# A channel mix in groups of four chunks, with the weights as the stationary operand in all three products

## The chip, the cores and the metric

The kernel runs on one core of a Trainium2 chip. The metric is the time of one execution on the device, in microseconds, of which the median of three runs is taken.

## The reference, cut to what matters

Inputs are q, k, v and a gate alpha, each 4 batches x 8 heads x 768 steps x 48 features, in fp32. A gated linear attention makes x (768 steps x 384 features a batch), and a channel mix follows it:

```python
for t in range(S):
    state = alpha[:, :, t, :, None] * state + np.einsum('bhd,bhe->bhde', k[:, :, t], v[:, :, t])
    y[:, :, t] = np.einsum('bhd,bhde->bhe', q[:, :, t], state)
...
x_prev = np.concatenate([np.zeros((B, 1, D)), x[:, :-1, :]], axis=1)
xk = mu_k * x + (1.0 - mu_k) * x_prev
xr = mu_r * x + (1.0 - mu_r) * x_prev
k = np.maximum(xk @ w_k, 0.0)          # 384 -> 1024, "up"
v = k * k @ w_v                        # 1024 -> 384, "down"
r = 1.0 / (1.0 + np.exp(-(xr @ w_r)))  # 384 -> 384, "gate"
return (r * v).astype(np.float32)
```

## The kernel before

The 3072 steps of all batches are cut into 24 chunks of 128 (six a batch). The attention works chunk by chunk, on data that DVE prepares in nine spans (PREP: three of two chunks, six of three): forward and backward scans of alpha (`scan` L826, `scan_back` L843), and products with q and k. On TensorE (PE) a chunk is a `visit`: scores of a later chunk (`sp`, masked by DVE into `am`, L983), transposes (`sp` L992, copied by ACT into `ht`), `intra` (L1023), `updates` (L1035, which DVE adds to the state `st`, L1062) and, for the chunk before, `inter` (L1049), all into the PSUM tile `yu`. ACT copies the result into `xt` (L1094), and SP's queue moves the features of a fourth row block into their place (`move_y3`, L1103).

The channel mix works on groups of chunks (MIX, before: three groups of two chunks and six of three, so 256 or 384 columns). Of a group, ACT and DVE first mix each step with the one before it (`x_mul`, `x_add`) and split the result in a high part (fp32r, by ACT) and a low part (by DVE). Then come, on PE:

- up: for each of eight blocks f of 128 hidden features, three tiles of input features times three factors (high x high, low weights x high, high x low), nine matmuls into one PSUM tile `pk` (L1160). The weights are stationary, the group's columns stream. ACT makes relu, DVE or ACT the square, ACT and DVE its high part `kh` and low part `kl`.
- gate: for each chunk, nine matmuls into `pg` (L1204). Here x is stationary (128 steps) and the 384 output features of the weights stream. ACT makes the sigmoid.
- down: for each chunk, 24 matmuls into `pv` (L1227), k stationary and the weights streaming. DVE multiplies with the sigmoid (`gated`, L1234), and SP stores 128 steps x 384 features (192 KB).

Group 0 (in FULL) is done in plain fp32 with one factor, each matmul as two instructions, while the weights are still being split for the rest. The PSUM tiles of the mix (`pm`) are two. A row of DVE's and ACT's work on a weight is `w_top`, `w_or`, `w_hi`, `w_lo` (L914 to L941).

Nothing is ordered by hand. `graph` builds a list of jobs with what they need and an estimated length; `SPOTS` says how many mix jobs on PE stand ahead of each visit; `Plan.run` sorts the jobs of the other engines by the length of what hangs on them, with an offset by kind and group from the table `SOONER`. The instructions of each engine, and the DMAs on SP's queue, are issued in that order, and each engine works strictly in order.

## Time and profile before

| what | value |
|---|---|
| median of three runs | 340.75 us (340.56 to 340.97) |
| span of the profiled execution | 339.2 us |
| PE busy | 327.1 us, 4552 matmul instructions |
| VectorE (DVE) busy | 242.4 us |
| ScalarE (ACT) busy | 193.5 us |
| mean granted TensorE clock | 0.997 |

The profile is one execution; its span runs from the first instruction of the program to the last, and its instruction times are what all sums below are made of. The median of the runs lies 1.6 us above that span. A busy time of PE counts each matmul from its start to the end of its pipeline, so matmuls in a row overlap, and the chain of work (which follows back what ended last) gives the spacing of matmuls better than their durations do.

### The profile page before, as it was taken

To read this page: it belongs to the slowest core of one execution; us is meant where nothing else is said; L and a number is where in the kernel's file an instruction comes from. 1 tells how busy PE (TensorE), PEld (TensorE's weight loads), DVE (VectorE), ACT (ScalarE), POOL (GpSimd) and SP (SyncE) were. 2 spreads that over 40 slices of the span, in tenths; PEclk is the share of its full clock that TensorE was granted. 3 is DMA by queue.
4 is the path that set the end of the run, shared out by engine and by line. 5 is a ranking of instruction groups with operands and counts; after the bars stand their busy time and mean duration, and the time that the engine had idled before them with its cause. 6 is when DMAs were issued, how large, how long until landed. Compare 5 with 4: busy or idle time off the path is not lost.

```text
span 339.2 us, 10688 instructions
## 1 busy us (share of the span) xinstructions
PE 327.1 (96%) x4552; PEld 307.6 (91%) x4552; DVE 242.4 (71%) x513; ACT 193.5 (57%) x439; POOL 6.8 (2%) x28
## 2 busy tenths in 40 slices
PE   8888999999999999999999999999999999999993
PEld 8777865799999999999999999999999999999992
DVE  4989998998985997788669965893667256627310
ACT  3586773587588396655554564752667167706400
POOL 5000000000000000000000000000000000000000
PEclk9999999999999999999999999999999999999998
DMA  7989493433434232414243215121000000010001
GB/s 225 409 334 278 154 336 95 146 97 131 134 89 163 47 106 85 148 39 137 70 162 79 75 33 182 43 56 52 14 10 23 32 31 9 23 47 2 2 23 53
DMA packets 14325, 35.38 MB, mean 104 GB/s; under 512 B 2432, under 2 KB 9344, under 8 KB 13504
## 3 DMA queue, kind: packets, MB, share of 16 engines
q1 hardware_dynamic: 14016, 33.73, 30.5%
q10 hardware_dynamic: 256, 0.92, 1.0%
q8 instruction: 37, 0.61, 0.7%
q14 instruction: 16, 0.13, 0.1%
HBM read 26.57 MB, written 4.72 MB: 92 GB/s over the span
## 4 chain that ended last, share of the span: by engine, by line
PE 80%; DVE 7%; DMA 6%; ACT 5%; issue 1%; DVEq 0%; ACTq 0%
PE pv L1227 29%; PE pk L1160 25%; PE pg L1204 10%; PE yu L1049 4%; PE sp L975 3%; PE yu L1023 3%; PE sp L992 3%; PE yu L1035 3%; DMA rv<-wv_p 2%; DMA al<-al_p 1%; DMA kq<-kq_p 1%; DVE pp L843 1%; DVE am L983 1%; DMA xt<-xt 1%; ACT xt L1094 1%
## 5 line engine op out<-in xcount | busy, mean ns | idle before, releaser
L1227 PE MATMUL pv<-wvh,kh 128*128 128x384 f32 x176 | 59.7, 339 | 0.2 <-DVE flag L1256 0.2
L1227 PE MATMUL pv<-wvh,kl 128*128 128x384 f32 x176 | 59.5, 338 | 0.0
L1227 PE MATMUL pv<-wvl,kh 128*128 128x384 f32 x176 | 59.3, 337 | 0.0
L1168 ACT ACTIVATE r<-pk 128x384 f32<-128x384 f32 (+1 forms) x72 | 32.6, 452 | 29.0 <-PE pk L1160 27.6
L1160 PE MATMUL pk<-xkh,wkh 128*128 128x384 f32 (+1 forms) x192 | 42.3, 328 | 0.0
L1160 PE MATMUL pk<-xkl,wkh 128*128 128x384 f32 (+1 forms) x192 | 41.4, 324 | 0.0
L1160 PE MATMUL pk<-xkh,wkl 128*128 128x384 f32 (+1 forms) x192 | 41.2, 323 | 0.0
L1193 DVE TENSOR_TENSOR kl<-k,kh 128x384 fp32r<-128x384 f32 (+1 forms) x64 | 33.1, 524 | 10.7 <-ACT k L1174 4.8
L1176 DVE TENSOR_TENSOR k<-r 128x384 f32<-128x384 f32 x48 | 26.6, 556 | 18.7 <-ACT r L1168 18.4
L1189 ACT ACTIVATE kh<-r 128x384 fp32r<-128x384 f32 (+2 forms) x72 | 35.1, 489 | 1.9
L1131 ACT ACTIVATE x<-xt,mu 128x384 f32<-128x384 f32 (+1 forms) x48 | 26.4, 584 | 13.8 <-DVE xkl L1144 11.0
L1227 PEld LDWEIGHTS pv<-wvh,kh 128*128 128x128 f32 x176 | 33.0, 188 | 0.3 <-DVE flag L1256 0.3
L1227 PEld LDWEIGHTS pv<-wvl,kh 128*128 128x128 f32 x176 | 33.1, 188 | 0.0
L1094 ACT COPY xt<-yu 48x256 f32<-48x256 f32 (+1 forms) x72 | 26.7, 371 | 11.1 <-PE yu L1049 10.2
L1227 PEld LDWEIGHTS pv<-wvh,kl 128*128 128x128 f32 x176 | 33.0, 188 | 0.0
L1160 PEld LDWEIGHTS pk<-xkh,wkh 128*128 128x128 f32 x192 | 32.1, 188 | 0.3
L1234 DVE TENSOR_TENSOR sig<-pv,sig 128x384 f32<-128x384 f32 x24 | 13.3, 554 | 26.6 <-PE pv L1227 26.6
L1160 PEld LDWEIGHTS pk<-xkh,wkl 128*128 128x128 f32 x192 | 32.2, 188 | 0.1
L1160 PEld LDWEIGHTS pk<-xkl,wkh 128*128 128x128 f32 x192 | 32.1, 188 | 0.1
L1135 DVE SCALAR_TENSOR_TENSOR x<-xt,nu,x 128x384 f32<-128x384 f32 (+1 forms) x48 | 26.4, 579 | 3.0 <-ACT x L1131 3.0
L826 DVE TENSOR_TENSOR_SCAN pp<-al,tiny 128x384 f32<-128x384 f32 (+2 forms) x28 | 22.7, 847 | 4.1 <-DMA al<-al_p 4.0
L843 DVE TENSOR_TENSOR_SCAN pp<-al,inv 128x384 f32<-128x384 f32 (+2 forms) x28 | 24.9, 914 | 0.0
(89 smaller groups left out, 514.1 us busy)
## 6 DMA issues: line engine op xcount, KB each, us to landing
kq<-kq_p SPq DMA_DIRECT2D x6, 1153.5 KB, 6.2
out<-sig SPq DMA_DIRECT2D x24, 192.0 KB, 1.9
al<-al_p SPq DMA_DIRECT2D x6, 577.5 KB, 4.1
v<-v_p SPq DMA_DIRECT2D x6, 576.0 KB, 4.6
rk<-wk_p SPq DMA_DIRECT2D x4, 768.0 KB, 8.5
rv<-wv_p SPq DMA_DIRECT2D x4, 768.0 KB, 5.2
kq<-kq_p SPq DMA_DIRECT2D x2, 769.5 KB, 8.6
v<-v_p SPq DMA_DIRECT2D x3, 384.0 KB, 8.1
```

What stands on the lines that cost most here:

```text
L826: self.DVE.tensor_tensor_scan(self.pp[g][:, t], self.al[g][:, t, :n], self.tiny[:rows].to_broadcast([rows, n]), initial=START, op0=ALU.mul ...
L843: self.DVE.tensor_tensor_scan(self.pp[g][:, t][:, ::-1], al, al, initial=self.inv[: rows_of(g), g, t : t + 1], op0=ALU.mult, op1=ALU.bypass,)
L1094: self.ACT.copy(self.xt_of(m)[dst, :, at + s * HB : at + (s + 1) * HB], self.yu[c][src, s, : NP * HB].rearrange("r (p t) -> r p t", p=NP),)
L1131: self.ACT.activation(x, xt[:, t, 1 : 1 + n], AF.Copy, scale=self.mu[:, i, t : t + 1])
L1135: self.DVE.scalar_tensor_tensor(x, xt[:, t, 0 : xt.shape[2] - 1], self.nu[:, i, t : t + 1], x, op0=ALU.mult, op1=ALU.add)
L1160: self.PE.matmul(pk, w[:, t, f * 128 : (f + 1) * 128], x[:, t], start=part == 0 and t == 0, stop=part == len(pairs) - 1 and t == NT - 1,)
L1168: self.ACT.activation(self.r[m, f], pk, AF.Relu)
L1176: self.DVE.tensor_tensor(k2, r, r, op=ALU.mult)
L1189: self.ACT.activation(self.khl_of(m)[0][:, f], self.r[m, f], AF.Square)
L1193: self.DVE.tensor_tensor(kl[:, f], self.k2[m, f], kh[:, f].bitcast(F32), op=ALU.subtract)
L1204: self.PE.matmul(pg, x[:, i, t * 128 : (t + 1) * 128], w[:, i], start=part == 0 and i == 0, stop=part == len(pairs) - 1 and i == NT - 1,)
L1227: self.PE.matmul(pv, x[:, f, cols], w, start=f == 0 and i == 0, stop=f == NF - 1 and i == len(pairs) - 1,)
```

## The change

Three things change. The groups of the mix are two of two chunks and then five of four (512 columns, one PSUM bank). Since six chunks make a batch, two of these groups straddle a batch's end, and their `xt` has two leading columns in place of one. In gate and down the operands are exchanged: 128 output features of the weights are stationary, and the group's columns stream; so there are three tiles of output features where there was one tile for each chunk, and the result stands by feature. The stores write it so (three of 128 features x 256 or 512 steps a group; 256 KB for a group of four), and the host turns it. The square's buffer becomes a ring of three in the place of a weight buffer, and the sigmoids of later groups go to two other freed weight buffers. Last, SPOTS and SOONER are new tables.

```diff
-MIX = [2, 2, 2, 3, 3, 3, 3, 3, 3]
+MIX = [2,2,4,4,4,4,4]
...
+def pieces_of(m):
+
+    cs = MG[m]
+    two = cs[0] // NCB != cs[-1] // NCB
+    assert not two or (len(cs) % 2 == 0 and cs[len(cs) // 2] % NCB == 0)
+    return 1 + two
...
+def sig_at(m):
+
+    return f"sg{m}" if m in (0, 1) else WHOLE_AT[m % 2 if type(m) is int else m[1] % 2]
...
 SPOTS = [
-    0, 0, 0, 0, 0, 0, 0, 0, 0, 0, 0, 0, 0, 5, 7, 7, 9, 10, 11, 11, 16, 20, 24, 33, 59, 65, 71,
-    103, 109, 115, 145, 151, 156, 185, 193, 201, 233, 240, 247, 269, 276, 290,
+    0, 0, 0, 0, 0, 0, 0, 0, 0, 0, 0, 0, 0, 3, 4, 4, 6, 7, 7, 7, 15, 16, 17, 22, 63, 68, 87, 116,
+    120, 123, 149, 153, 163, 190, 198, 213, 243, 246, 285, 290, 298, 299,
 ]
...
 SOONER = {
-    "carry 0": 20, "carry 1": -34.5, "carry 2": 29, "carry 4": -0.5, "carry 5": 20,
+    "carry 0": 34, "carry 1": -15, "carry 2": -60, "carry 3": 60, "carry 4": 36.5, "carry 5": 40,
...
-                  [r] + ([k2_used[-2]] if len(k2_used) > 1 else []))
+                  [r] + ([k2_used[-3]] if len(k2_used) > 2 else [raw_of["raw2"]]))
...
-        for t in range(n // C):
+        for t in range(NT):
...
-                p = J("PE", 3 * mm(DM), L("gate", m, t, 0), busy + [w[0] for w in ws] + [xh[1, i] for i in range(NT)])
+                p = J("PE", 3 * mm(n), L("gate", m, t, 0), busy + [w[0] for w in ws] + [xh[1, i] for i in range(NT)])
...
-            sig[t] = J("ACT", act(DM), L("sigmoid", m, t), [p2] + ([sig_use[-4]] if len(sig_use) > 3 else []))
+            sig[t] = J("ACT", act(n), L("sigmoid", m, t), [p2] + sig_room(m))
...
-        for t in range(n // C):
+        for t in range(NT):
             slot, busy = take()
             prev = None
-            for f in range(0, NF, 2):
+            for f in range(NF):
...
+    def sig_room(m):
+
+        at = sig_at(m)
+        if at not in WHOLE_AT:
+            return []
+        if sig_at(m - 2) == at:
+            return [sig_use[m - 2, i] for i in range(NT)]
...
+    def x_parts(self, m, t, late):
+
+        xt, two = self.xt[m], self.two[m]
+        w = xt.shape[2] // two
+        x = xt[:, t]
+        if two == 1:
+            return x[:, 1:] if late else x[:, : w - 1]
+        x = x.rearrange("r (s w) -> r s w", s=two)
+        return x[:, :, 1:] if late else x[:, :, : w - 1]
...
     def gate(self, m, t, part):
...
         for i in range(NT):
             self.PE.matmul(
-                pg, x[:, i, t * 128 : (t + 1) * 128], w[:, i],
+                pg, w[:, i, t * 128 : (t + 1) * 128], x[:, i],
...
-    def down(self, m, t, f0):
+    def down(self, m, t, f):
...
+            self.PE.matmul(
+                pv, w[:, cols], x[:, f],
+                start=f == 0 and i == 0, stop=f == NF - 1 and i == len(pairs) - 1,
+            )
...
     def store(self, m, t, eng):
-        at = (MG[m][0] + t) * C
-        self.queue[eng].dma_start(self.out[at : at + C], self.sig.pop((m, t)))
+        at = MG[m][0] * C
+        sig = self.sig[m][:, t]
+        self.queue[eng].dma_start(self.out[t * 128 : (t + 1) * 128, at : at + sig.shape[1]], sig)
...
-    return r.results[0]["out"].reshape(B, S, DM)
+    return r.results[0]["out"].reshape(DM, B, S).transpose(1, 2, 0)
```

What the tables do to the order is seen at two places. The first is PE's order where the down matmuls of group 0 (`pv<-wv`, in fp32) end and the up matmuls of group 1 (`pk` with `wkh`, `wkl`) begin; `sp<-kq` are scores and `yu<-am` the intra part of a visit. Before:

```order
L1227 MATMUL pv<-wv_649,kh 128x384 x4
L1227 MATMUL pv<-wv_468,kh 128x384 x4
L975 MATMUL sp<-kq_444 64x64 x12
L975 MATMUL sp<-kq_0_80 64x64 x4
L1227 MATMUL pv<-wv_649,kh 128x384 x4
L1160 MATMUL pk<-xkh,wkh 128x256 x3
L1160 MATMUL pk<-xkh,wkl 128x256 x3
L1023 MATMUL yu<-am_795,v_379 64x64
```

Here chunk 4's visit (the last row is its start) follows the first six up matmuls of group 1. The same place after, with the end of chunk 6's visit in its first two rows:

```order
L994 MATMUL sp<-kq_1_81 64x64 x4
L1011 MATMUL sp<-ident,kq_453 128x128 x3
L1268 MATMUL pv<-kh,wv_598 128x256
L1268 MATMUL pv<-kh,wv_799 128x256 x4
L1268 MATMUL pv<-kh,wv_598 128x256 x4
L1268 MATMUL pv<-kh,wv_799 128x256 x4
L1198 MATMUL pk<-xkh,wkh 128x256 x3
L1198 MATMUL pk<-xkh,wkl 128x256 x3
L1198 MATMUL pk<-xkl,wkh 128x256 x3
L1198 MATMUL pk<-xkh,wkh 128x256 x3
```

The visits of chunks 4, 5 and 6 have moved ahead, into the down matmuls of group 0, and group 1's 72 up matmuls follow each other without a visit.

The second place is DVE's order where the states of chunk 4 (`st`) stand beside the forward scans of span 4 (`pp<-al,tiny`); `am` is a mask, `wvl`, `wkl` and `wv` are work on weights, `x` and `xkl` mixing, `sig` the product of a finished tile. Before:

```order
L826 SCALAR_TENSOR_TENSOR pp_880<-al_818,tiny 128x384
L1234 TENSOR_TENSOR sig<-pv,sig 128x384
L826 SCALAR_TENSOR_TENSOR pp_880<-al_818,tiny 128x384 x2
L1062 TENSOR_TENSOR st_0_953<-yu,st_1_748 112x192
L983 TENSOR_TENSOR am_960<-sp,mask 128x512
L1062 TENSOR_TENSOR st_1_970<-yu,st_0_953 112x192
```

Chunk 4's first state follows the scans, which have a product between them. After:

```order
L1002 TENSOR_TENSOR am_842<-sp,mask 128x512
L845 SCALAR_TENSOR_TENSOR pp_846<-al_791,tiny 128x384 x3
L1081 TENSOR_TENSOR st_0_908<-yu,st_1_750 112x192
L1002 TENSOR_TENSOR am_910<-sp,mask 128x512
L1081 TENSOR_TENSOR st_1_913<-yu,st_0_908 112x192
L960 TENSOR_TENSOR wkl<-wk_202,wkh 128x3x256
L942 SCALAR_TENSOR_TENSOR wv_799<-rv_837,tops_85 128x768
```

The three scans now stand in one row ahead of the state, and the low parts of the weights (`wkl`) that were done before them have moved behind.

## Rows read from the trace of the kernel before

**Rows 1.** The page's head: span, then busy time, share and instructions of engines.

```profile
span 339.2 us, 10688 instructions
...
PE 327.1 (96%) x4552; PEld 307.6 (91%) x4552; DVE 242.4 (71%) x513; ACT 193.5 (57%) x439; POOL 6.8 (2%) x28
```

**Rows 2.** Stretches (us): length, busy time of each engine (instructions), granted clock, DMA share, GB/s.

```profile
40.00:60.00 20.00, 19.40 (x308) 12.66 (x307) 18.21 (x37) 10.73 (x25) 0.46 (x1) 1.00 0.67 221
60.00:80.00 20.00, 19.69 (x460) 17.15 (x460) 19.26 (x43) 15.26 (x44) 0.40 (x1) 1.00 0.49 154
80.00:100.00 20.00, 20.00 (x344) 19.61 (x344) 17.65 (x42) 13.52 (x37) 0.00 (x0) 1.00 0.26 72
...
180.00:240.00 60.00, 60.00 (x816) 58.50 (x818) 45.28 (x94) 32.13 (x71) 0.10 (x1) 1.00 0.25 74
240.00:300.00 60.00, 60.00 (x742) 58.67 (x731) 34.35 (x67) 35.37 (x77) 0.32 (x1) 1.00 0.06 19
```

**Rows 3.** PE's waits: what waited for whom, us in total, times, longest.

```profile
PE pb L958 <- POOL ident masks.py:199: 1.6, 1, 1.6
PE yu L1049 <- DVE st L1062: 0.9, 2, 0.6
PE pk L1160 <- ACT r L1168: 0.8, 1, 0.8
```

**Rows 4.** The chain that ended last, in order of time: start, us, what.

```profile
91.66 1.06 PE pk L1160 x9
...
97.20 0.59 PE yu L1049 x32
...
99.65 2.12 PE pk L1160 x18
...
104.23 3.18 PE pk L1160 x27
...
285.58 4.76 PE pg L1204 x27
290.34 12.63 PE pv L1227 x72
302.98 12.48 PE pk L1160 x72
```

**Rows 5.** DVE's groups by form: busy us, mean ns of one, idle time before and releasers.

```profile
L983 DVE TENSOR_TENSOR am<-sp,mask 128x512 f32<-128x512 f32 x24 | 16.6, 690 | 11.4 <-ACT ht L1000 5.8 <-PE sp L992 5.0 <-PE sp L975 0.5
L826 DVE TENSOR_TENSOR_SCAN pp<-al,tiny 128x384 f32<-128x384 f32 x18 | 16.4, 944 | 0.0
...
L1062 DVE TENSOR_TENSOR st<-yu,st 112x192 f32<-112x192 f32 x40 | 14.1, 352 | 6.8 <-PE yu L1035 6.7
...
L1234 DVE TENSOR_TENSOR sig<-pv,sig 128x384 f32<-128x384 f32 x24 | 13.3, 554 | 26.6 <-PE pv L1227 26.6
```

**Rows 6.** DMA issues: queue, operation, count, KB each, median us from issue to landing.

```profile
out<-sig SPq DMA_DIRECT2D x24, 192.0 KB, 1.9
al<-al_p SPq DMA_DIRECT2D x6, 577.5 KB, 4.1
v<-v_p SPq DMA_DIRECT2D x6, 576.0 KB, 4.6
...
xt<-xt SPq DMA_DIRECT2D x48, 24.0 KB, 2.5
```

**Rows 7.** DVE's timeline from 64 to 91 us: start, us, line, operation, count.

```profile
64.17 0.96 DVE L826 TENSOR_TENSOR_SCAN pp<-al,tiny 128x384 f32<-128x384 f32 x1
...
67.20 0.34 DVE L1062 TENSOR_TENSOR st<-yu,st 112x192 f32<-112x192 f32 x1
...
90.39 0.43 DVE L1144 TENSOR_TENSOR xkl<-x,xkh 128x256 fp32r<-128x256 f32 x1 [0.15 <-ACT xkh L1140]
```

**Rows 8.** ACT's timeline within group 1's up matmuls, columns as in the group above.

```profile
79.31 0.37 ACT L1168 ACTIVATE r<-pk 128x256 f32<-128x256 f32 x1
...
80.34 0.37 ACT L1168 ACTIVATE r<-pk 128x256 f32<-128x256 f32 x1
```

111 lines of the change are left out of this document (62 added, 49 removed), and 135 rows, old and new, of the table SOONER.

## The prediction

> **What bounds the kernel now.** I read the page's head first: TensorE (PE) is busy for 327.1 of 339.2 us [rows 1]. That share proves nothing by itself, since matmuls overlap, so I went to the table of stretches: from 80 to 100 us and again from 180 to 300 us PE has no idle time at all, at a granted clock of 1.00, the 2.4 GHz level, while VectorE (DVE) is at 18 to 19 of each 20 us between 40 and 100 us and has a quarter or more to spare later [rows 2]. The list of PE's waits agrees: it has ten entries, 5.9 us together, the longest of 1.6 us [rows 3]. So from 80 us to the last matmul the time is the sum of PE's own matmuls. Every matmul saved there shortens the run by its full spacing, and every microsecond by which the early part hands over later lengthens it by the same. Before that PE waits now and then, for DVE, ScalarE (ACT) and loads.
>
> **What a matmul costs.** A matmul's duration in the profile contains the pipeline; the spacing is what counts, and the chain shows it, since PE runs there without a break [rows 4]. Up with 256 columns: 27 in 3.18 us, 117.8 ns each. Up with 384: 72 in 12.48 us, 173.3 ns. Gate: 27 in 4.76 us, 176.3 ns. Down: 72 in 12.63 us, 175.4 ns. Of three-factor matmuls before there are 144 up of 256, 432 up of 384, 198 gates and 528 downs: 17.0 + 74.9 + 34.9 + 92.6 = 219.4 us.
>
> After the change group 1 still has 256 columns: 72 up, 27 gate and 72 down matmuls, 171 x 117.8 ns = 20.1 us. Five groups of 512 columns have 72 + 27 + 72 each, 855 in all. The columns streamed are the same; 1302 instructions become 1026. Group 0 runs in plain fp32: 6 gate and 16 down matmuls of 384 become 9 and 24 of 256, the same columns, two instructions each. Those are 22 instructions more (44 to 66), at 13 ns beyond their columns 0.3 us at most. I take 0, since PE waits in that stretch anyway.
>
> No 512-column matmul stands in the trace, so it is bounded by the two widths that do. Straight through 117.8 and 173.3 gives 0.434 ns per column and **228.8 ns** at 512. If a column takes one cycle of 2.4 GHz and all the rest of the 384-column up (173.3 - 160 = 13.3 ns) is per instruction, it is 226.6 ns. If the whole cost goes with columns, up is 231.1 ns, and gate and down, at 4/3 of about 175.4, are 233.9. The line rests on two rows, the others on one each, so I take the line: 855 x 228.8 = 195.6 us, with group 1 215.7 us, a gain of **3.6 us** (5.5 us at one end, 219.1 us in all and a gain of 0.3 us at the other). All of it falls after group 2 starts, where PE is the limit.
>
> The rows of both widths lie over columns / 2.4 GHz by 11.1 and 13.3 ns. The Trainium skill, page "TensorE: Matmul & The Clock Gate", section "Back-to-back issue gap", gives a warm gap of N/2.4 + 2.5 ns, thus 109.2, 162.5 and 215.8 ns; the trace disagrees at both widths, by 8.6 and 10.8 ns, and the measurement decides. By the Trainium skill's figure for 512 alone the sum would be 204.6 us; by its 2.5 ns per instruction alone the 276 instructions saved would be worth 0.7 us.
>
> **Tail.** The last down tile is followed by its product with the gate and by a store. At 512 columns the product is like the mask's 128x512 read of PSUM, 690 against 554 ns [rows 5]: +0.14 us. The store grows from 192 to 256 KB, in rows of 2 KB. That costs between nothing and 64 KB at the slope from 192 KB in 1.9 us to 576 KB in 4.6 us [rows 6], 0.45 us; I take 0.25, between. Tail **+0.4 us**.
>
> **Middle.** Relu, square, high and low part and the mix become fewer and wider, on ACT and DVE, which have 25% to 46% to spare from 180 to 300 us [rows 2]; the cover is PE itself, some 2.06 us for nine matmuls, against two DVE instructions (square and low part) of about 0.69 us each. The second group of 512 and the later ones must have four chunks of attention evacuated before their mix; the order puts the last of these visits before or early in the preceding group's down matmuls, of which at least 48 of 512 columns (11.0 us) or, for group 2, 72 of 256 and a visit (10.9 us) still follow. Three copies, the 2.5 us move [rows 6] and the mixing of three tiles (twelve instructions of 0.6 to 0.7 us on two engines) are some 8 us, shorter than this. I cost it at nothing; with that cover gone it would be those 8 us a group. The new waits are long past when they come: a sigmoid waits for stores two groups back, a square for the low part three back in place of two. On SP's queue the load of span 4's k and q now stands behind group 0's first store and so behind its product; the multiplications that need it come twenty DVE instructions after that product, so it has time to land.
>
> **The early part.** This is where the change can lose. In the old order groups 2 and 3 need chunks 4, 5 and 6 to 8; now group 2 needs chunks 4 to 7, so two visits of attention more (and a third, chunk 9's, by the new order) stand ahead of its first up matmul. A visit takes 2.45 us of PE (97.20 to 99.65 us) and group 2 started at 91.7 us [rows 4], so with the same pace it starts at 91.7 + 3 x 2.4 = 98.9 us, and as that PE work is only moved it costs nothing. The question is whether DVE gets there. By that point it now has to do in addition three masks (0.69 us), six states (0.35), one rescaling (two instructions like a state's, 0.7), the forward scans of the next span (three at 0.94 [rows 5]) and wider mixing: six instructions at 512 columns (0.69, as the mask) in place of seven at 256 (0.43 [rows 7], the adds a little more), 1.0 us. That is 8.6 us. In the old order its work ahead of group 2 ended with a low part at 90.8 us [rows 7]; 90.8 + 8.6 = 99.4 us. PE needs this last result only for the third factor, six matmuls (1.4 us) behind the start, at 100.3 us. It fits on the sum, by 0.9 us, with DVE at 18.2, 19.3 and 17.7 of each 20 us from 40 to 100 us [rows 2], so with some idle time of its own left.
>
> What fits less well is the order inside. The visits of chunks 4 to 6 now stand in group 0's down matmuls and no longer between group 1's up matmuls (the first order excerpt). DVE works in order, and in both orders the state for chunk 4's inter matmul stands behind three forward scans of span 4 (the second excerpt; 64.17 to 67.20 us before [rows 7]). In the old order PE had scores, transposes and twelve up matmuls (1.4 us) to do in the meantime and still waited, one of the two waits for states, 0.9 us together [rows 3]. Now one fp32 down matmul replaces the twelve, two instructions of 256 columns, twice 117.8 ns at the least: the wait grows by 1.0 to 1.2 us. The scans themselves need a load that is issued when span 3's backward scans free its buffer and takes 4.1 us [rows 6]; if DVE comes to them early it stands still, with masks, states and high/low splits queued behind, and PE waits for those. Further, group 1's 72 up matmuls now run without a visit between: ACT's relu, high part and square come every 1.03 us (79.31 to 80.34 us [rows 8]) against 1.06 us of PE for nine matmuls, so anything else on ACT's queue ahead of a relu, such as a tile of mixing, shows in full. Against that, the old order lost 0.8 us to a relu and the 0.9 us to states [rows 3], which the new one may avoid. Bounds: -1.7 us (those stalls gone) to +4 us (the scans' load, the state and ACT, one behind the other). I take **+1.0 us**, the growth of the one wait that can be followed.
>
> **The sum.** 339.2 - 3.6 + 0.4 + 1.0 = 337.0 us of span. The median of the runs (340.75) is 1.6 us over the profiled span, so **338.5 us**, 0.66% faster.
>
> **Rivals.**
> 1. *The cost goes with the columns.* Fewer instructions bring 0.3 us only, and tail and early part remain: 339.2 - 0.3 + 0.4 + 1.0 + 1.6 = 341.9 us, or 340.9 without the early loss. For it: gate and down, with other operands but the same columns, cost 2 to 3 ns more than up, so something beyond a fixed cost per instruction is there. Against it: 256 columns cost 0.460 ns each and 384 cost 0.451, so width did help once.
> 2. *The early stretch becomes the bound* (slower). DVE, in order, holds the states of chunks 4 to 7 behind scans that wait for a load, and group 2 starts at 103 us or later in place of 98.9. It decides from 3.9 us on, where the gain less the tail (3.2 us) and 0.7 us beyond are used up. With 5 us: 339.2 - 3.6 + 0.4 + 5.0 + 1.6 = 342.6 us. For it: DVE is the fullest engine beside PE there, and PE stalls for single waits of that kind already. Against it: the sums leave 0.9 us, and PE's single waits are under 1 us after the first [rows 3].
> 3. *The excess vanishes at 512.* At 213.3 ns (512 columns at 2.4 GHz) the matmuls take 202.5 us, a gain of 16.9 and 325.2 us in all. Against it: the excess grew from 256 to 384. The Trainium skill's gap above (same page and section) would give 204.6 us, thus 327.4 us; at 256 and 384 columns the trace disagrees with it.
>
> **Chances.** Forecast, with the per-instruction end of its band, 0.72; rival 1 0.12; rival 2 0.13; rival 3 0.03. A measurement of this kernel tells about 0.2% (0.7 us) from no change: faster means below 340.1, slower above 341.4 us. Forecast: 0.67 faster, 0.05 same. Rival 1: 0.06 same, 0.06 slower. Rival 2: 0.03 same, 0.10 slower. Rival 3: 0.03 faster. Together 0.70, 0.14, 0.16. The range runs from 335.0 us (226.6 ns and 1.6 us of the old early stalls gone: 339.2 - 5.5 + 0.4 - 0.6 + 1.6) up to 342.0 us, which takes in rival 1 and half of rival 2.
>
> **What would show it.** In the trace after: 72 up matmuls of 512 columns on the chain in 16.3 to 16.6 us (228.8 ns each), the same spacing in gate and down; a first 512-column matmul at 98 to 101 us; from there no PE wait over 0.5 us; after the last matmul 0.7 us of DVE and a store of 2.0 to 2.3 us. It is wrong if the spacing is over 231 or under 226 ns, if group 2 starts past 102 us, or if PE waits at the head of a later group.

## The result, and the profile after

The changed kernel took 342.33 us (median of seven runs, 341.74 to 345.19) against 340.91 us of the kernel before beside it: a ratio of 1.0071, with an interval from 1.0046 to 1.0095. It is 0.7% slower, where 338.5 us and 0.66% faster were forecast, and lies 0.3 us over the upper end of the range. The profiled execution took 341.74 us. The head of its page answers [rows 1]:

```profile
span 340.0 us, 10014 instructions
...
PE 323.8 (95%) x4298; PEld 272.4 (80%) x4298; DVE 232.9 (68%) x454; ACT 186.5 (55%) x380; POOL 7.5 (2%) x28
```

Every engine beside GpSimd has less to do, and the span is 0.8 us longer (340.0 against 339.2). The stretches, as [rows 2] (length, busy time of each engine, granted clock, DMA share, GB/s), show on which side of 100 us that happens:

```profile
40.00:60.00 20.00, 17.68 (x345) 14.23 (x344) 18.62 (x38) 14.91 (x35) 0.23 (x2) 1.00 0.68 209
60.00:80.00 20.00, 19.11 (x337) 17.73 (x338) 19.65 (x43) 12.18 (x32) 0.00 (x0) 1.00 0.45 129
80.00:100.00 20.00, 19.49 (x482) 18.78 (x482) 16.25 (x36) 12.59 (x33) 0.19 (x1) 1.00 0.31 91
...
180.00:240.00 60.00, 60.00 (x831) 49.35 (x830) 37.41 (x71) 29.82 (x60) 0.41 (x3) 1.00 0.20 59
```

From 40 to 100 us PE is idle for 2.32 + 0.89 + 0.51 = 3.72 us; before it was 0.91 us [rows 2]. From 100 to 300 us it is never idle. Of PE's waits over the run (what waited for whom, us in total, times, longest) these are the largest beside the start's:

```profile
PE yu L1068 <- DVE st L1081: 2.4, 2, 1.9
...
PE sp L994 <- DVE am L1002: 1.3, 1, 1.3
PE pv L1268 <- DVE wv L942: 1.3, 1, 1.3
```

The same list for the stretch from 101 us to the end has one entry:

```profile
PE pv L1268 <- DVE flag L1298: 0.2, 1, 0.2
```

PE's timeline has the start of group 2, the third group, before and then after:

```profile
91.49 0.51 PE L1160 MATMUL pk<-xkh,wkh 128*128 128x256 f32 x3
```

```profile
101.54 0.63 PE L1198 MATMUL pk<-xkh,wkh 128*128 128x512 f32 x2
```

The first up matmul of 512 columns starts at 101.54 us. Before, the group of that place started at 91.49 us (the 91.66 us of [rows 4] are the chain's, which counts a piece from the end of the one ahead), and the three visits moved ahead of it measure 2.28 us each, so 98.3 us would have been level: the early part lost **3.2 us**. From there to the last matmul it is 232.3 us; before it was 333.5 - 91.5 = 242.0 us, of which 6.8 us are the three visits. The later part gained **2.9 us**. After the last matmul come 6.2 us in place of 5.7: **0.5 us**. -2.9 + 3.2 + 0.5 = +0.8 us, the difference of the spans. The medians differ by 1.4 us; executions of the changed kernel run from a mean granted clock of 0.996 (341.74 us) down to 0.987 (345.19 us), and the profiled one is the former.

**The matmuls.** PE's timeline at the last group (start, us, line, operation, count) gives the spacing from start to start:

```profile
293.50 0.85 PE L1198 MATMUL pk<-xkh,wkh 128*128 128x512 f32 x3
...
309.97 0.85 PE L1245 MATMUL pg<-xrh,wrh 128*128 128x512 f32 x3
...
332.70 0.40 PE L1268 MATMUL pv<-kl,wvh 128*128 128x512 f32 x1
332.94 0.40 PE L1268 MATMUL pv<-kh,wvh 128*128 128x512 f32 x1
333.18 0.40 PE L1268 MATMUL pv<-kh,wvl 128*128 128x512 f32 x1
```

72 up matmuls take 309.97 - 293.50 = 16.47 us, 228.8 ns each, as forecast. Gate follows with the same 0.69 us for three. Down does not: its matmuls follow each other by 0.24 us, and 72 of them, where nothing comes between, take 16.92 us, 235 ns each.

**The early waits.** DVE's timeline from 37 to 60 us, and PE's two waits that follow from it:

```profile
37.92 0.55 DVE L942 SCALAR_TENSOR_TENSOR wr<-rr,tops 128x384 uint32<-128x384 uint32 x1
...
46.02 0.95 DVE L942 SCALAR_TENSOR_TENSOR wv<-rv,tops 128x768 uint32<-128x768 uint32 x1
...
54.81 0.96 DVE L942 SCALAR_TENSOR_TENSOR wv<-rv,tops 128x768 uint32<-128x768 uint32 x1 [1.38 <-ACT tops L933]
55.69 0.87 DVE L1173 SCALAR_TENSOR_TENSOR x<-xt,nu,x 128x256 f32<-128x256 f32 x2
56.48 0.68 DVE L1002 TENSOR_TENSOR am<-sp,mask 128x512 f32<-128x512 f32 x1
57.08 2.65 DVE L845 TENSOR_TENSOR_SCAN pp<-al,tiny 128x384 f32<-128x384 f32 x3
59.65 0.33 DVE L1081 TENSOR_TENSOR st<-yu,st 112x192 f32<-112x192 f32 x1
```

```profile
55.83 0.70 PE L1268 MATMUL pv<-kh,wv 128*128 128x256 f32 x2 [1.27 <-DVE wv L942]
...
60.89 0.67 PE L1068 MATMUL yu<-kq,st 48*48 48x64 f32 x32 [1.89 <-DVE st L1081]
```

`wv` is a quarter of the down weights, put together by DVE (`w_or`) from what a load (`rv`) and ACT (`tops`) bring; group 0's down matmuls need these quarters in turn. The third comes 1.3 us too late for PE, and DVE itself waits 1.38 us for it. The mixing, the mask, three scans and the state behind it are late with it, and PE waits 1.89 us for that state. PE had come out of the quarter's wait late itself, so the 1.89 us are not that delay once more: the three scans ahead of the state alone take 2.57 us. In the old order the wait for chunk 4's state was short:

```profile
68.46 0.66 PE L1049 MATMUL yu<-kq,st 48*48 48x64 f32 x32 [0.26 <-DVE st L1062]
```

Up to the start of group 2 PE is idle for 9.7 us in all, before for 6.0 us. Of the 3.7 us more, 0.9 lie before 40 us (among the waits there is that of 1.28 us for a mask, up to 37.27 us; ahead of that mask DVE had waited 0.87 us for the load of span 2's k and q), 0.7 at the quarter (before, one such wait of 0.60 us), 1.6 at chunk 4's state and 0.5 at a state at 88.4 us. PE's own work up to there is 0.5 us shorter, which leaves the 3.2 us.

The quarters are late from the load on. SP's queue, before and then after (start, us for the issue, count):

```profile
24.81 0.33 SPq L882 DMA_DIRECT2D rv<-wv_p  x1
31.90 7.51 SPq L882 DMA_DIRECT2D rv<-wv_p  x2
46.80 0.33 SPq L882 DMA_DIRECT2D rv<-wv_p  x1
```

```profile
29.50 0.38 SPq L901 DMA_DIRECT2D rv<-wv_p  x1
...
38.50 0.33 SPq L901 DMA_DIRECT2D rv<-wv_p  x1
...
47.00 0.33 SPq L901 DMA_DIRECT2D rv<-wv_p  x1
...
55.80 0.33 SPq L901 DMA_DIRECT2D rv<-wv_p  x1
```

DVE's row of the last gate weight before:

```profile
31.29 0.55 DVE L923 SCALAR_TENSOR_TENSOR wr<-rr,tops 128x384 uint32<-128x384 uint32 x1
```

The loads of the first three quarters are issued at 24.8, 31.9 and 39.1 us before (the second row holds two) and at 29.5, 38.5 and 47.0 us after. The second waits for a buffer that the last gate weight (`wr`) leaves. DVE made that one at 31.29 us before and makes it at 37.92 us now, behind scans of span 2 that the new tables put first. The later quarters share one buffer, so each load starts when the last quarter is put together, and a link (load, ACT, DVE) takes 8.5 us for the second and 8.8 us for the third.

### The profile page after: what moved, and what is told of

Its sections match the earlier page's. It is cut to its first block, busy times and chain, and to the rows that moved or that the text cites. A ratio compares the mean times of both kernels' runs of the same rounds, so it can differ in the third digit from the quotient of the medians.

```text
span 340.0 us, 10014 instructions
## 1 busy us (share of the span) xinstructions
PE 323.8 (95%) x4298; PEld 272.4 (80%) x4298; DVE 232.9 (68%) x454; ACT 186.5 (55%) x380; POOL 7.5 (2%) x28
## 5 line engine op out<-in xcount | busy, mean ns | idle before, releaser
L1268 PE MATMUL pv<-kh,wvh 128*128 128x512 f32 (+1 forms) x144 | 55.0, 382 | 0.2 <-DVE flag L1298 0.2
L1268 PE MATMUL pv<-kl,wvh 128*128 128x512 f32 (+1 forms) x144 | 54.2, 376 | 0.0
L1268 PE MATMUL pv<-kh,wvl 128*128 128x512 f32 (+1 forms) x144 | 54.0, 375 | 0.0
L1206 ACT ACTIVATE r<-pk 128x512 f32<-128x512 f32 (+1 forms) x56 | 29.9, 533 | 26.2 <-PE pk L1198 24.8
L1198 PE MATMUL pk<-xkh,wkh 128*128 128x512 f32 (+1 forms) x144 | 38.6, 377 | 0.0
L1198 PE MATMUL pk<-xkh,wkl 128*128 128x512 f32 (+1 forms) x144 | 38.4, 375 | 0.0
L1198 PE MATMUL pk<-xkl,wkh 128*128 128x512 f32 (+1 forms) x144 | 38.2, 374 | 0.0
L1230 ACT ACTIVATE kh<-r 128x512 fp32r<-128x512 f32 (+2 forms) x56 | 31.7, 569 | 1.3
L1234 DVE TENSOR_TENSOR kl<-k,kh 128x512 fp32r<-128x512 f32 (+1 forms) x48 | 30.2, 644 | 3.0 <-ACT k L1215 0.4
L1268 PEld LDWEIGHTS pv<-kl,wvh 128*128 128x128 f32 x144 | 27.1, 188 | 5.5
```

Of the source, the lines that this page charges most:

```text
L1198: self.PE.matmul(pk, w[:, t, f * 128 : (f + 1) * 128], x[:, t], start=part == 0 and t == 0, stop=part == len(pairs) - 1 and t == NT - 1,)
L1206: self.ACT.activation(self.r[m, f], pk, AF.Relu)
L1230: self.ACT.activation(self.khl_of(m)[0][:, f], self.r[m, f], AF.Square)
L1234: self.DVE.tensor_tensor(kl[:, f], self.k2[m, f], kh[:, f].bitcast(F32), op=ALU.subtract)
L1268: self.PE.matmul(pv, w[:, cols], x[:, f], start=f == 0 and i == 0, stop=f == NF - 1 and i == len(pairs) - 1,)
```

## The experiments

e1 to e3, e5 and e15 to e18 move single steps within one engine's row of the order (shown as the step and what it now stands ahead of); from e4 on, but for e5, e6 and e8, the edit of e4 is in. "Third" is when the third quarter of the down weights is put together, "start" that of the first 512-column matmul, both in the profiled execution.

Ratios are to runs of the kernel before on the same chip at the same time.

| run | median us (range) | ratio to before | span | third | start |
|---|---|---|---|---|---|
| after | 342.33 (341.74 to 345.19) | 1.0071 [1.0046, 1.0095] | 340.0 | 55.8 | 101.54 |
| e1 | 343.66 (342.43 to 345.58) | 1.0083 [1.0055, 1.0111] | 342.3 | 56.1 | 103.00 |
| e2 | 342.89 (342.02 to 344.65) | 1.0071 [1.0046, 1.0096] | 340.8 | 56.2 | 102.53 |
| e3 | 344.77 (343.37 to 345.35) | 1.0116 [1.0096, 1.0137] | 341.7 | 56.3 | 103.67 |
| e4 | 342.16 (339.94 to 344.30) | 1.0035 [1.0014, 1.0057] | 338.9 | 55.9 | 101.54 |
| e5 | 346.84 (345.70 to 347.99) | 1.0188 [1.0162, 1.0214] | 344.0 | 59.5 | 105.66 |
| e6 | 349.27 (348.49 to 350.05) | 1.0248 [1.0215, 1.0282] | 348.0 | | |
| e7 | 346.60 (345.56 to 347.41) | 1.0165 [1.0141, 1.0190] | 345.2 | 57.2 | 106.79 |
| e8 | 342.05 (341.38 to 343.49) | 1.0042 [1.0027, 1.0057] | 340.4 | | |
| e9 | 344.25 (343.85 to 347.30) | 1.0132 [1.0101, 1.0164] | 342.2 | 56.2 | 104.78 |
| e10 | 354.46 (353.93 to 355.05) | 1.0408 [1.0386, 1.0430] | 353.1 | 59.2 | 114.42 |
| e11 | 358.68 (357.30 to 359.46) | 1.0531 [1.0503, 1.0559] | 357.0 | 58.9 | 119.53 |
| e12 | 342.62 (340.45 to 344.99) | 1.0059 [1.0030, 1.0088] | 339.9 | 55.1 | 102.57 |
| e13 | 340.90 (339.67 to 342.04) | 1.0006 [0.9986, 1.0025] | 338.4 | 53.4 | 100.94 |
| e14 | 341.50 (339.53 to 342.25) | 1.0012 [0.9995, 1.0030] | 339.7 | 56.6 | 102.33 |
| e15 | 342.18 (339.80 to 344.85) | 1.0042 [1.0015, 1.0069] | 341.0 | 56.3 | 103.53 |
| e16 | 342.28 (341.49 to 343.94) | 1.0054 [1.0032, 1.0076] | 339.7 | 56.3 | 102.36 |
| e17 | 340.78 (339.84 to 341.50) | 0.9999 [0.9988, 1.0010] | 339.7 | 55.6 | 101.74 |
| e18 | 344.16 (342.82 to 346.66) | 1.0117 [1.0086, 1.0148] | 343.0 | 59.0 | 105.56 |

**Weights and scans moved (e1, e2, both in e3).** e1 puts the weights' loads and their work earlier, e2 two of the three scans behind the state:

```diff
+    (('load_w', ('v', 0, 'SP')), ('load_kq', (3, 0, 3, 'SP'))),
+    (('load_w', ('v', 1, 'SP')), ('load_kq', (3, 0, 3, 'SP'))),
+    (('w_or', ('r', 1)), ('scan', (2, 0))),
...
+    (('scan', (4, 1)), ('w_lo', ('k', 0))),
+    (('scan', (4, 2)), ('w_lo', ('k', 0))),
```

> The changed kernel with one chain of loads moved forward and nothing else. In its trace the last piece of the gate weights is put together by VectorE at 37.92 us, behind span 2's scans, though ScalarE had its part ready at 29.65; that frees the buffer into which v's pieces are loaded one by one (38.50, 47.00, 55.80 us), and TensorE waits 1.49 us at 54.34 for piece 2. Here that step stands ahead of the scans, and the loads and unpacking of pieces 1 and 2 move up with it. Theory A (the early part is lost to single waits that an order can take away): the wait at 54.34 goes, piece 2 is ready near 53.4, and 1.2 to 1.5 us reach the end: first 512-column up matmul near 100.1 in place of 101.54, span 338.5 to 338.9, median of executions at the full clock near 340.3. Rival B (VectorE's sum is the bound before group 2, single waits are only where it shows): the gain is taken back by 100 us, the first 512-column matmul stays at 101.3 to 101.6, span 339.8 to 340.1.

> The changed kernel with two of span 4's three forward scans (0.88 us each) moved on VectorE from ahead of chunk 4's states to behind the assembly of v's last piece; nothing else. In the changed kernel PE waits 2.27 us at 58.63 for the state behind these scans. Theory A: the state comes 1.0 us sooner (58.7 in place of 59.65, as its own input is ready at 58.4), the wait shrinks to about 1.3 us, and v's last piece (ready at 62.57 in the changed kernel, near 62.1 here) is just in time for what follows: gain 0.7 to 1.0 us, first 512-column up matmul near 100.7, span near 339.1. If the weight's load is the real bound there, a new wait of 0.5 us or more opens at the sixth feature's down matmul, and the gain is under 0.5 us. Rival B (VectorE's sum): the scans' 1.8 us come back as a later wait, first 512-column matmul at 101.3 to 101.9, span 339.9 to 340.4.

> Both edits of the two kernels before it. Theory A: their gains add, since the first removes the load as the next thing that is late: 1.4 + 1.0 = 2.2 to 2.6 us, first 512-column up matmul at 98.9 to 99.4 (where the prediction had it, 98.9), span 337.4 to 337.9. Rival B (VectorE's sum is the bound before group 2): well under 1 us together, first 512-column matmul past 100.8, span 339.2 or more.

All three are slower than the changed kernel in the span. In e1 PE's wait for the third quarter is gone, though the quarter comes no sooner (56.1 us): PE is late itself, after a longer wait some seven microseconds ahead of that place, here on DVE and then on PE:

```profile
43.27 1.81 DVE L845 TENSOR_TENSOR_SCAN pp<-al,tiny 128x384 f32<-128x384 f32 x2 [1.94 <-DMA al<-al_p]
```

```profile
48.83 0.67 PE L1068 MATMUL yu<-kq,st 48*48 48x64 f32 x32 [2.90 <-DVE st L1081]
```

The two quarters' loads, now ahead of that of span 3's k and q, put it back (landed at 40.8 us, in after at 36.2), and behind it the load of span 3's decay (issued at 36.8 us, landed at 43.2, in after at 41.0), which the scans need. A second wait for a state, of 2.11 us, follows at 62.45 us. In e2 the wait for the state falls from 1.89 to 1.19 us, but PE then waits 0.65 us for scores at 67.8 us, and the start comes 1.0 us later all the same. So theory A failed in all three: each wait taken away came back as another. Since e1 moved loads too, it doesn't tell DVE's order from the loads.

**Down's operands by factor (e4).** Up takes all tiles of one factor before the next; down alternates the factors f by f. e4 does down by factor:

```diff
+            row = [(w, x, i) for w, x in ((wh, kh), (wl, kh), (wh, kl)) for i in range(NF)]
```

> The changed kernel with another order inside down in the five groups of 512 columns: the eight high-by-high matmuls of a tile first, then the eight with the weights' low part, then the eight with the input's low part, as up and gate have it (there three of each), in place of the three factors one behind the other for each feature block. Same matmuls, same operands. Theory C (the order in which operands change sets the spacing): down falls from 235 to 238 ns to the 229 to 230 of up and gate, 360 x 6 = 2.2 us, span 337.8. Theory D (the spacing belongs to the operands themselves, where they lie and how they were written, whatever stands before): down stays at 234 to 238 ns and the span within 0.3 us of 340.0.

PE's timeline in the last group's down matmuls (eight a row):

```profile
317.93 2.02 PE L1273 MATMUL pv<-kh,wvl 128*128 128x512 f32 x8
319.79 2.00 PE L1273 MATMUL pv<-kl,wvh 128*128 128x512 f32 x8
321.62 2.00 PE L1273 MATMUL pv<-kh,wvh 128*128 128x512 f32 x8
```

Eight take 1.83 to 1.86 us, 229 to 232 ns each, and 72 undisturbed ones 16.70 us (231.9 ns) in place of 16.92. All 360 take 84.6 us in place of 85.4. The start of the 512-column groups stays at 101.54 us and the span of the profiled execution falls by 1.1 us; the runs don't tell the two apart (the intervals of the ratios overlap). So about half of the excess of unbroken down rows over up is the order of the operands, and neither theory is right as it stands.

**A load put off (e5).** The load of span 3's k and q, issued at 28.87 us in after, is issued later, directly ahead of that of its decay (at 37.4 us).

> The changed kernel with one load moved on SP's queue: span 3's k and q (1153 KB) are issued behind span 2's move (near 36.9 us) and no longer at 28.87 us, where they share the DMA queues with span 2's k and q (issued at 26.36) and v's first piece (29.50). The three kernels with moved steps showed group 2 starting later by about as much as VectorE's idle time ahead of it grew (0.43 more idle, 0.99 later; 1.04 and 1.46; 1.97 and 2.13). Theory B (VectorE is the bound from 28 us to the states of chunk 8 near 87 us, so only its idle time counts): span 2's load lands near 31.7 in place of 32.9, VectorE's 0.87 us of idle time there goes, PE's wait of 1.66 us at 35.6 shrinks to 0.8, and the first 512-column up matmul comes at 100.6 to 100.9 in place of 101.54, unless v's pieces now come later. If the load was held up by something else than its neighbours, nothing moves (101.4 to 101.7).

Its span is 4.0 us longer than after's. The second quarter's load lands at 47.5 us in place of 44.5. PE waits 1.88 us, from 45.8 us on, within its scores and 0.93 us more for a state, and then the clock falls: 0.73 in the stretch from 44 to 52 us, where instructions of plain fp32 matmuls of 256 columns follow each other by 427 ns in place of 216.

**The turned operands at the old groups (e6).** Groups and spots near those of before, weights stationary, the order not searched for it:

```diff
-MIX = [2,2,4,4,4,4,4]
+MIX = [2, 2, 2, 3, 3, 3, 3, 3, 3]
```

> The changed kernel's operand orientation (weights stationary in gate and down, output by feature) with the old groups of two and three chunks, the old table of priorities, and the old places of the visits carried over to the new rows. Its order is not searched, so its time tells little (341 to 347 us); the spacing is the question. If turning the operands is itself what costs in down, down with 384 columns is at 179 ns or more (the old orientation has 175.4). If width is the cause (235 at 512 where up has 229), down with 384 columns stays at 175 to 177 ns. Gate should come to up's 173.3 from 176.3, as its weights are now stationary as in up.

Gate costs 173.3 ns at 384 columns (before 176.3) and down 175.5 (175.4): turning the operands costs nothing there. The time itself says little, since the order is unfit: a wait of 1.91 us for a quarter of the down weights, then half the clock (length, busy times, granted clock):

```profile
55.00:58.00 3.00, 1.09 (x6) 0.64 (x5) 2.21 (x4) 1.77 (x6) 0.00 (x0) 1.00 0.07 17
58.00:61.00 3.00, 3.00 (x8) 2.38 (x9) 3.00 (x6) 0.91 (x2) 0.48 (x1) 0.51 0.23 41
```

**An order searched with slower loads (e7, e8).** The plan lets a load land by its size alone; in the trace of after the four quarters, 768 KB each, took 4.2 to 8.8 us. Both kernels, changed (e7) and before (e8), got tables searched by a plan with slower loads:

```diff
-                finish = max(finish, dma + self.LAND)
+                finish = max(finish, dma + self.LAND, s + 0.6 + 2.4 * jobs[i][4] / self.BW)
```

> The changed kernel with down by factor and with its order searched anew, with a load taken to land after 0.6 us and 2.4 times its transfer at 390 GB/s, at least (5.2 us for a piece of v, 7.7 for a span's k and q, as in the traces; the plan had 3.9 and 4.8). By that rule the old order of the changed kernel has group 2 at 102.7 us (the trace: 101.54) where the plan it was searched with has 97.2. If loads that land later than planned are what was lost (theory E), group 2 starts at 98.0 to 99.5 and the span is 335.5 to 337.5. If not, it starts past 100.5 and the span is over 338.

> The kernel before, old orientation and groups, with its order searched anew in the same way and for as long. By the same rule its old order has group 2 at 92.6 us (the trace: 91.49), the new one at 87.6. Theory E gives a group 2 at 87.5 to 89.0 and a span of 335.5 to 337.0. If the old order was as good as this stretch lets it be, nothing moves (338.5 to 339.5). Beside the run before it this tells what the new groups are worth with orders made by the same rule: by the sums of matmuls 2.5 us in their favour, less what four chunks ahead of the first wide group cost.

Neither gained: e7 is 4.4 us over e4, e8 0.4% over before (its group 2 starts at 91.58 us, where 87.5 to 89.0 was expected). This guess of the loads found no better order for either; another might. Side by side, with orders made by one rule, the new groups are 4.5 us slower than the old (346.60 against 342.05 us), though the sums of matmuls favour them; with one search each, how lucky a search was is not known. In e7 the loads were pressed together (DMA share 0.98 from 30 to 40 us), PE waited three times between 37 and 44 us (1.61, 1.79 and 0.69 us), and the clock was 0.50 from 44.0 to 49.4 us.

**Waits filled with matmuls (e9, e14).** Small matmuls of the identity into an unused part of `yu` stand where PE waits: ten at each of three waits (e9), four at each of the two near 55 and 60 us (e14).

```diff
+        for _ in range(FILL):
+            self.PE.matmul(
+                self.yu[c][:, 0, 448:512], self.ident, self.ident[:, :HB], start=False, stop=True, skip_group_check=True
+            )
```

> The changed kernel with down by factor, and ten small matmuls (128 x 64, into unused columns of PSUM, result not read) put at each of PE's three long waits: ahead of chunk 3's scores (a wait of 1.7 to 2.0 us at 35.6), of group 0's fifth down (1.3 to 1.5 us at 54.5) and of chunk 4's inter (2.3 us at 58.7). Ten such take 0.6 to 1.1 us, so they fit into the waits. Theory G (in some executions these waits let the clock fall to 1.2 GHz for some 5 us, as the kernel with the old groups shows behind a wait of 2.3 us and the one with the new order behind waits of 2.1 and 0.9 us, and that makes the changed kernel's slower executions): the clock of all executions is 0.994 or more, their spread falls from 4.4 us (339.9 to 344.3 with down by factor alone) to under 2 us, and the median from 342.2 to 340.3 to 341.0; the profiled span stays at 338.7 to 339.3. Rival H (the spread comes from loads that land earlier or later): spread and median stay where they are.

> The changed kernel with down by factor, with four unread matmuls (0.21 us each in the kernel with all waits filled, 0.85 us together) in each of two waits, at 54.5 (1.3 to 1.5 us) and 58.7 us (2.3 us), now into a part of PSUM that no one is still to read, so that they run within the wait. Theory G (these waits let the clock fall in some executions): group 2 stays at 101.4 to 101.8 in the profiled one, the clock of all executions is 0.994 or more, their spread is under 2.5 us, the median 340.3 to 341.2 (342.2 with down by factor alone). Rival H: spread 3 to 4.5 us and median 342.0 or more, clocks between 0.988 and 0.997 as before.

e9 put in too much: a 64-column fp32 matmul is two instructions of some 0.1 us, so ten are 2.1 us, longer than the waits; and the last ten waited 1.18 us for the state themselves, so they ran behind that wait. With four, the fill lies inside the wait:

```profile
55.32 1.10 PE L982 MATMUL yu<-ident 128*128 128x64 f32 x8
56.68 0.70 PE L1286 MATMUL pv<-kh,wv 128*128 128x256 f32 x2 [0.26 <-DVE wv L943]
```

e14 has a median 0.7 us below e4's and its highest run 2.0 us below, though its profiled span is not shorter (339.7 against 338.9). No step comes earlier. What it takes away is the long end of the runs. This is weak by itself: the intervals of the two ratios overlap, and e14 lies a little outside theory G's band at each point (start 102.33 us, spread 2.7 us, median 341.50 us, one run at a clock of 0.990), though nearer to it than to rival H's. e16 and e17 below are the better pair.

**Work taken from DVE (e10, e11, e12, e13).** e10 lets GpSimd make eight low parts of weights, e11 does that and fills waits. e12 leaves out three products of span 3's q, e13 all twelve of k and q in spans 2 and 3:

```diff
+        eng = self.POOL if (key, f) in ON_POOL else self.DVE
...
+        if g in (3,):
+            return
```

> The changed kernel with down by factor, and eight of the ten subtractions that make the weights' low parts moved from VectorE to GpSimd, which is idle there; all other rows keep their order. They are 0.55 to 0.95 us each on VectorE, 0.95 us ahead of chunk 4's states and 6.3 us between 60 and 83 us. Theory B (VectorE's work in order is the bound until 87 us): the waits behind it shrink, as far as no load takes over: the one at 58.6 not or by little (what was ahead of it was followed by idle time), those from 60 to 90 us (1.5 to 2 us together) all. Group 2 at 99.5 to 100.8 in place of 101.54, span 337.0 to 338.3 (338.9 with down by factor alone). If GpSimd takes over 3 us for one, or slows VectorE where both work, group 1's second factor waits for it and group 2 starts at 101.5 or later.

> Down by factor, the waits filled and the low parts on GpSimd. If theories B and G both hold: span 337.0 to 338.3, spread under 2 us, median 338.7 to 340.0, faster than the kernel before (340.8). If only G holds: median 340.3 to 341.0. If neither: 342 and a spread of 4 us.

> The changed kernel with down by factor, leaving out the three multiplications of span 3's q by the decay (0.5 us each on VectorE, 43.3 to 45.8 us), so 1.55 us of VectorE's work and nothing else; part of the output is then not the reference's. Theory B (VectorE in order is the bound up to chunk 4's states at 59.65 us): everything behind it on VectorE comes up to 1.55 us sooner, v's pieces 1 to 3 with it, group 2 at 100.0 to 100.5 in place of 101.54. Rival E (the loads are the bound: v's pieces 2 and 3 take 6.3 us each from issue to landing): VectorE idles longer ahead of v's second piece (1.4 us before) and group 2 comes at 101.0 to 101.6.

> The same with all twelve multiplications of spans 2 and 3 left out (k and q, 5.2 us of VectorE's work between 33 and 52 us). Theory B: group 2 starts 2.5 to 3.2 us earlier, at 98.3 to 99.0, which is where PE's own work ends when it never waits (98.3, from the kernel before's 91.49 and three visits of 6.83), and the span is 335.7 to 336.4 where down by factor alone has 338.9. Rival E (the loads): VectorE's idle time grows by most of the 5.2 us and group 2 comes at 100.5 or later.

e10 and e11 are far slower. GpSimd's and then DVE's timeline in e10:

```profile
56.55 4.33 POOL L962 TENSOR_TENSOR wkl<-wk,wkh 128x768 fp32r<-128x768 f32 x2
...
80.38 3.98 POOL L962 TENSOR_TENSOR wvl<-wv,wvh 128x768 fp32r<-128x768 f32 x2
```

```profile
56.92 2.27 DVE L943 SCALAR_TENSOR_TENSOR wv<-rv,tops 128x768 uint32<-128x768 uint32 x1 [1.39 <-ACT tops L934]
59.11 2.45 DVE L1175 SCALAR_TENSOR_TENSOR x<-xt,nu,x 128x256 f32<-128x256 f32 x2
...
82.62 0.26 DVE L856 TENSOR_SCALAR kq<-pp 128x1 f32<-128x1 f32 x3
82.81 1.97 DVE L871 TENSOR_TENSOR kq<-kq,pp 128x384 f32<-128x384 f32 x1
```

While GpSimd subtracts, the quarter takes 2.27 us in place of 0.96, two adds 2.45 in place of 0.87 and a product 1.97 in place of 0.54, all with two tiles to read; three small instructions with one take their usual 0.26 us.

e12 and e13 take 1.55 and 5.2 us off DVE's work. The third quarter comes 0.7 and 2.4 us sooner than in after, yet the start moves by +1.0 and only -0.6 us. PE's wait for chunk 4's state in e13:

```profile
58.84 0.66 PE L1072 MATMUL yu<-kq,st 48*48 48x64 f32 x32 [2.17 <-DVE st L1085]
```

This is 2.2 us sooner than in e4 (61.02 us). Links of e13 still take 8.0 us, and DVE's idle time from 26 us up to chunk 4's state grows from 2.4 us (e4) to 4.4: part of what was taken away is lost in waits for loads, for ACT and for PE, and 2.2 us reach PE. So neither DVE's work alone nor the loads alone set the pace there. Then in both the clock falls after the wait, which costs 1.6 us: by the next visit's inter matmuls the 2.2 us are down to 0.6 (65.04 us in e13, 65.63 in e4). Here the stretch from 60 to 64 us of after, e13 and e14 in turn:

```profile
60.00:64.00 4.00, 3.11 (x119) 2.96 (x120) 4.00 (x7) 2.19 (x4) 0.00 (x0) 1.00 0.18 21
```

```profile
60.00:64.00 4.00, 4.00 (x55) 3.56 (x51) 2.49 (x5) 1.28 (x4) 0.00 (x0) 0.57 0.57 159
```

```profile
60.00:64.00 4.00, 2.95 (x122) 2.75 (x121) 4.00 (x7) 2.19 (x4) 0.00 (x0) 1.00 0.05 16
```

**The chain of quarters once more (e15 to e18).** e15 moves the first quarter's load ahead of span 3's k and q; e16 shortens the chain by moves on DVE, ACT and SP; e17 is e16 with one fill of four; e18 gives the third quarter a buffer of its own, so that its load starts at 39.3 us.

```diff
+    (('load_w', ('v', 0, 'SP')), ('load_kq', (3, 0, 3, 'SP'))),
...
+    (('w_or', ('r', 1)), ('x_add', (0, 1, 1))),
+    (('w_or', ('v', 1)), ('scan', (3, 2))),
+    (('state', (3, 0)), ('scan', (3, 2))),
...
+        raw = self.raw[key, f] = self.p1.tile([128, 4 * w + 2], U16, tag="xrl" if (key, f) == ("v", 2) else RAW_AT[key, f], name=f"r{key}{f}")
```

> The changed kernel with down by factor, with the issue of v's first piece (0.38 us) put ahead of that of span 3's k and q on SP's queue (28.87 us), the small version of the edit that went too far when it put span 3 behind span 2's move. Theory E: span 2's k and q share the queues with one load less for about a microsecond and land 0.2 to 0.5 us sooner, VectorE's idle 0.87 us shrinks by that, group 2 at 101.0 to 101.4. If that load's neighbours do not matter at this scale: 101.4 to 101.7 and the same median as with down by factor alone (342.2).

> The changed kernel with down by factor, and the steps that end with v's third piece put together moved up a little each, without a load moved ahead of another before 45 us: the last gate piece (VectorE 37.9 us) ahead of two of the mix's adds, the second piece's top half (ScalarE 44.6) ahead of a copy, its assembly (VectorE 46.0) and chunk 3's states ahead of one scan, the third piece's load (SP 47.0) ahead of two moves; and two adds of the next mix behind chunk 4's states. In the traces without a fall of the clock, group 2 started 45.6 to 45.8 us after the third piece was put together (55.77 and 101.54; 55.9 and 101.54; 56.62 and 102.33 us). Theory E' (that chain sets group 2's start): third piece at 53.4 to 54.4 us, group 2 at 98.9 to 100.3, span 336.5 to 337.8, executions without a fall of the clock 338.2 to 339.6. Rival: PE or VectorE get in the way before (a new wait over 0.7 us at 44 to 52 us), the piece still comes at 55.5 or group 2 still at 101 or later.

> The same with four unread matmuls (0.85 us) in the wait ahead of chunk 4's inter. Theories E' and G: group 2 as in the run without them, all clocks 0.994 or more, spread under 2.5 us, median 338.4 to 339.6, faster than the kernel before (340.7). If the wait there is now shorter than 0.85 us, group 2 comes later by the difference, at most 0.8 us.

> The changed kernel with down by factor, the wait ahead of chunk 4's inter filled as in the run before, and v's third piece loaded into a buffer of its own (a tile that is free until group 1), so that its load is issued behind the second's (near 39 us in place of 47.0) and the fourth's where the third's was (near 47 in place of 55.8); its assembly stands ahead of a low part, ScalarE's part of the fourth ahead of span 4's relu. VectorE's work is the same. Theory E' (the chain of v's pieces through one buffer sets group 2's start): third piece at 53.2 to 53.8 us, fourth by 60, group 2 at 99.0 to 100.2, span 336.6 to 337.8, median 338.3 to 339.6, faster than the kernel before (340.7). If VectorE's order is the bound whatever the loads do: the idle 1.4 us ahead of the third piece goes, but group 2 still starts at 101 us or later. If the earlier load holds up others (span 3's decays, issued at 37.0): a new idle time of VectorE over 1 us near 43 us, and group 2 at 101.5 or later.

None brought the third quarter forward by more than 0.2 us. In e15 the clock fell from 62 to 66 us. In e16 the load of the second quarter follows that of span 3's decay by 0.7 us in place of 1.5; the decay landed at 43.0 us, in after at 41.0, DVE waited 1.00 us for it, and PE waited 0.96 us for a state, up to 47.54 us. The third quarter's load then landed sooner than in after (52.0 against 53.7 us) and ACT's part was done at 53.67 us, but DVE came to it only at 55.38 us, with no pause from 48.3 us on. ACT's and then DVE's timeline:

```profile
52.61 1.06 ACT L933 ACTIVATE tops<-rv 128x768 f16<-128x768 bf16 x1
```

```profile
53.39 1.47 DVE L875 TENSOR_TENSOR kq<-kq,pp 128x384 f32<-128x384 f32 x3
54.78 0.69 DVE L1002 TENSOR_TENSOR am<-sp,mask 128x512 f32<-128x512 f32 x1
55.38 0.95 DVE L942 SCALAR_TENSOR_TENSOR wv<-rv,tops 128x768 uint32<-128x768 uint32 x1
```

So where the load is sooner, DVE's work in order holds the quarter at about the same time. In e18 the two loads side by side held up the move of k and q issued right after them, and PE's scores waited for it:

```profile
48.11 0.61 PE L1003 MATMUL sp<-kq 48*64 48x64 f32 x8 [2.26 <-issue]
```

From 48 to 54 us the clock was then 0.50, and the third quarter came at 59.0 us, though its load had landed at 47.85 us: DVE waited 4.20 us for ACT's part. e17 is the best of the changed kernels that compute all of the output: level with before, 1.5 us under e16 by the fill alone (their intervals don't overlap), with a range of 1.7 in place of 2.5 us; the 338.4 to 339.6 us that theories E' and G together named were not reached. No version beat the kernel before.

**What the runs show together.** Where the clock stayed up around 60 us (after, e2, e4, e14, e16, e17), the start follows the third quarter by 45.6 to 46.4 us; where it fell there (e12, e13, e15), by 47.2 to 47.6 us. I read the first interval as the fixed work between, and the second as that plus 1 to 2 us of half clock. That is a regularity and no proof: e1, e3 and e9 kept their clock and have 46.9, 47.4 and 48.5 us (e9 with its long fills), and no run brought the third quarter forward by 3 us and left everything else alone.

## Why the prediction was wrong, step by step

**Right.** Up at 228.8 ns, and gate too: the straight line through 256 and 384 columns held at 512. The middle at nothing: no PE wait over 0.2 us after the start. Group 0 at nothing: it goes on in a stretch with waits, as before. The tail: 0.5 us against 0.4, with the product at 0.69 us. Rival 3 is refuted, and rival 1 for up and gate.

The Trainium skill, page "TensorE: Matmul & The Clock Gate", section "Back-to-back issue gap", gives N/2.4 + 2.5 ns as the warm gap of an isolated matmul, 215.8 ns at 512 columns, and about 131 ns for a stream of them. The trace's stream disagrees with the first by 13 ns, more than at the narrower widths, and with the second by some 98 ns.

**Mis-sized: down.** The term 855 x 228.8 ns took down like up, though its own row stood 2 ns above up's [rows 4]. All 360 down matmuls took 85.42 us, breaks for visits included, where 360 x 228.8 is 82.4: 3.0 us more, some 2.2 of them (6.2 ns each, as in the 72 unbroken ones) where nothing breaks them. 0.9 us of that is the order of the operands (e4). What the rest is stays open. The prediction's own sign of being wrong, a spacing over 231 ns, came true here. A gain that the sum left out hid this: the chain's rates are of unbroken rows, and a row that a visit breaks costs more. Before, 432 up matmuls stood in 20 pieces and took 77.7 us, 2.8 more than 432 x 173.3 ns; after, 360 stand in nine and take 83.5 us, 1.1 more than 360 x 228.8. So 2.9 us were gained where 3.6 were forecast.

**Failed: the early part.** The step is "I take +1.0 us, the growth of the one wait that can be followed". The early part lost 3.2 us. That wait did grow, for the reason given, but by 1.6 us in place of 1.0 to 1.2: from 0.26 to 1.89 us (the 0.6 us of [rows 3] belong to another wait, at 17.65 us). And other waits, which the step had at nothing, grew by 2.1 us: 0.7 for a quarter of the down weights, 0.9 before 40 us and 0.5 at a later state. The bound of the early part was made from DVE's sum of work and from one load, and the loads of the down weights were not followed. The tables moved DVE's `wr` 6.6 us back, and with it the buffer, the second quarter's load, and the chain of one buffer behind that. So DVE stood still 1.38 us ahead of the very scans whose delay the step had weighed, and the start came at 101.54 us where 98 to 101 was named. "It fits on the sum, by 0.9 us" did not decide: what was late were single steps, and of the 5.2 us that e13 took from DVE's sum 2.2 reached chunk 4's inter matmuls and, after a fall of the clock, 0.6 the start. That the waits arose so is read from the rows; how much of the 3.2 us each cause is worth is not shown, since each run that took one wait away opened another.

Two slips of the working change little: the visits were priced at 2.45 us from the chain and measure 2.28, and the five terms of DVE's additional work add up to 8.7, not 8.6 us.

**The rival that came true** is the second, in a smaller size and by another load: a loss of 3.2 us, under the 3.9 from which it was to decide alone, met a gain of 2.9 less 0.5. Its mechanism (DVE in order, states behind what waits for a load) is what the rows show at the third quarter; the scans' own load was there in time.

**The median** lies 2.3 us over the profiled span, not 1.6. The profiled execution itself lies 1.7 us over its span; the other 0.6 us are that most executions are longer than it. They differ by 3.5 us, the longer ones at a lower mean clock, and filling a wait took 1.5 us off the median (e17 against e16). The fall itself is seen in the profiles of e12, e13 and e15, not in one of the changed kernel as it stands, so for that kernel it is inferred. It isn't the whole either: the two fastest runs of e4 (339.94 and 340.29 us) have a mean clock of only 0.991.

**Open.** Whether this change can be had without the early loss. Four moves of loads (e1, e5, e16, e18) each put back another load or move, in stretches where the DMA share of after is 0.85 (20 to 40 us) and 0.68 (40 to 60 us) already, and in e16 and e17 a quarter that was loaded sooner met DVE still at other work.

## What to carry to other kernels

When a change makes a later part cheaper and moves work ahead of it, follow every load whose buffer is freed by a moved step, link by link, since a sum of engine time can fit and the chain be late; then follow what stands ahead of the load's user on its engine, since either can come last. Cost an operand order that has not run from its own nearest row, not from its neighbour's, and cost rows broken by other work apart from unbroken ones. Short waits of TensorE can cost twice, once as a wait and once as clock (1.6 us more in e13); a filler of a few small matmuls inside the wait is a cheap way to find out.
